# Cosine attention and a gated two-layer product on one Trainium2 core: the last key group's value products in 64 rows, beside the next pair's scores

## The chip, the cores and the metric

The kernel runs on one core of one Trainium2 chip. The metric is the device time of one execution in microseconds (us); a lower one is better. A profile of one execution stands beside it, in which the engines are called PE (TensorE, matrix products), PEld (its loads of stationary operands), DVE (VectorE), ACT (ScalarE), POOL (GpSimd) and SP (SyncE, which issues DMAs). L433 means line 433 of the kernel before.

## What is computed

The inputs are q, k and v of 8 batches, 12 heads, 448 positions and 64 columns, and two weight matrices of 768 x 2048 and 2048 x 768. The reference, cut to what matters:

```python
q_n = q / (norm(q) + 1e-06);  k_n = k / (norm(k) + 1e-06)
scores = matmul(q_n, k_n.T) / tau              # tau = 0.1
attn = exp(scores - max) / sum(exp(scores - max))
x = matmul(attn, v)                            # heads side by side: 3584 x 768
h = x @ w_in
out = (h * clip(h + 3, 0, 6) / 6) @ w_out      # 3584 x 768
```

## The kernel before

The work goes by **pairs** of heads: pair i is batch i // 6 and two heads of it, A and B; there are 48 pairs. Operands of TensorE are bf16, sums are float32 in PSUM.

*Scores* (`scores`, L394) are made transposed: keys stand on the partitions, the 448 queries along the free axis. The 448 keys of a head fall into three blocks of 128 and a rest of 64, which makes four groups of a pair: `GROUPS = [("A0","B0"), ("A1","B1"), ("A2","B2"), ("M",)]`. In groups 0 to 2, each head's product has a contraction of only 64 (the head's columns); A's stands in rows 0 to 63 of the array and B's in rows 64 to 127. Group 3, "M", holds the last 64 keys of both heads, A's on partitions 0 to 63 and B's on 64 to 127; its scores are one product over all 128 rows (from pair 6 on). So a pair then has seven score products, and each takes one PSUM bank.

*Exponentials* (`exps`, L412): ScalarE reads each bank and writes a tile `at` in bf16, seven instructions a pair. Its columns 448 to 511 are set to 1.

*Values* (`values`, L433): the stationary operand is a block of `at`, 128 keys by 128 queries, and the moving one is a block of `vx`, 128 keys by 65 columns: 64 columns of v and a column of ones, whose product is the softmax's sum. There are four blocks of queries, j = 0 to 3. Groups 0 to 2 take eight matmuls of 65 columns each. Group 3 takes four matmuls of 130 columns over all 128 rows: its two blocks of `vx` (slots 3 and 4) hold A's last keys on rows 0 to 63 and zeros below, and zeros above B's on rows 64 to 127. All four groups add up in `PV`, two PSUM banks: bank j // 2 holds two blocks of queries, each with A's 65 columns and B's. `finish_values` (L453, L454, VectorE) divides by the sums and writes `on` in bf16; DMA transposes bring it to `xT`.

*The two layers* run as units between the pairs: `mm1_unit` (L513: six matmuls of 448 columns into a bank, then ACT's relu at L522 and DVE's product at L528 into `gT`) and `mm2_unit` (L549: sixteen matmuls of 384 columns, copied out by ACT at L560 or by DVE at L562 in turn, then stored by DMA).

*The order* of every engine's instructions is written out by hand: an engine takes them in the order in which the program's calls stand. A written list (PLAN) covers pairs 0 to 17, with matmuls on zeros (L615, L620) that fill gaps. From pair FIRST = 18 on a loop does the same for each pair: the next pair's scores of groups 0 to 2, their exponentials, the previous pair's values of groups 1 to 3, `finish_values`, the score and exponential of group 3, the units, with the preparation of later pairs among them, and at the end the pair's own values of group 0.

*The banks.* Two banks are PV's. The six others form a ring that scores and units share in the order of their use (`next_bank`): the first six scores of a pair take all six, the seventh takes the bank of the first again, the first unit after it that of the second. A matmul that opens a bank waits until the last reader of its former content is done.

Of the kernel before, what the change touches and what calls it, by code (L numbers as in the profile page):

```python
# [17 lines left out]
FIRST = 18  # L18
# [43 lines left out]
def kernel(  # L62
# [10 lines left out]
    nc = tc.nc  # L73
    B, H, S, D = q.shape
# [3 lines left out]
    HP = H // 2  # L78
    NP = B * HP
# [50 lines left out]
    PV = psum.tile([128, 2, 512], FP32, name="PV", tag="PV")  # L130
# [13 lines left out]
    def needs(*what):  # L144
        for w in what:
            assert w in issued or any(x < 0 for x in w[1:] if isinstance(x, int)), w
# [217 lines left out]
    GROUPS = [("A0", "B0"), ("A1", "B1"), ("A2", "B2"), ("M",)]  # L364
# [46 lines left out]
            o = at[:, 0 : len(GROUPS[g]), 0:S] if len(x.shape) == 3 else at[:, n, 0:S]  # L411
            nc.scalar.activation(out=o, in_=x, func=AF.Exp, scale=inv_tau)  # L412

    def pv_out(j):
        return PV[:, j // 2, 0:260].rearrange("p (j h e) -> p j h e", j=2, h=2)[:, j % 2, :, :]


    def q_cols(b, j):
        return slice(128 * j, 128 * j + 128)

    def values(i, g):
        needs(("VC", i), ("FI", i - 1), *([("VA", i, g - 1)] if g else []))
        at = at_of.pop((i, g))
        vt = vx[i % NVX]
        last = g == len(GROUPS) - 1
        for n, name in enumerate(GROUPS[g]):
            for j in range(4):
                if name == "M":
                    o, mv = pv_out(j), vt[:, 3:5, :]
                else:  # L430
                    h = "AB".index(name[0])
                    o, mv = pv_out(j)[:, h, :], vt[:, 5 * h + int(name[1]), :]
                nc.tensor.matmul(  # L433
                    o,
                    at[:, n, q_cols(i // HP, j)],
                    mv,
                    start=(name == "A0" and j % 2 == 0),
                    stop=last,
                    skip_group_check=True,
                )  # L440

    twin_on = {}

    def finish_values(i):
        needs(*(("VA", i, g) for g in range(4)))
        if i % 2 == 0:
            needs(("BK", i - 4), ("BK", i - 3))
            twin_on[i // 2] = sb.tile([128, 2, 4, 2, D], BF16, name="on", tag="on", bufs=2)
        rc = sb.tile([128, 2, 4], FP32, name="rc", tag="rc", bufs=2)
        on = twin_on[i // 2][:, i % 2, :, :, :]  # L450
        on_of[i] = on
        pv4 = PV[:, :, 0:260].rearrange("p b (n e) -> p b n e", e=D + 1)
        nc.vector.reciprocal(out=rc[:, :, :], in_=pv4[:, :, :, D])  # L453
        nc.vector.tensor_tensor(  # L454
            out=on[:, :, :, :].rearrange("p (b j) h d -> p b (j h) d", b=2),
            in0=pv4[:, :, :, 0:D],
            in1=rc[:, :, :].to_broadcast([128, 2, 4, D]),
            op=ALU.mult,
        )
# [178 lines left out]
    def whole_units(n):  # L638
# [7 lines left out]
        "LQ": load_qk, "LV": load_v, "W": next_weights, "SQ": square, "RE": reduce, "NO": norms,  # L646
        "NM": normalise, "VC": vcast, "TR": transposes, "XD": crossbar, "XB": back_crossbar, "XP": back_two, "CQ": copy_q, "CK": copy_k, "CS": copy_k3, "SC": scores,
        "EX": exps, "VA": values, "FI": finish_values, "BK": back, "CX": copy_x, "U": unit, "UA": lambda: finish_units("a"), "UV": lambda: finish_units("v"),
        "UU": whole_units, "D": busy, "DP": busy_pv, "OPEN": open_ring,
    }  # L650

    def do(op, *args):
        OPS[op](*args)
        key = (op,) + tuple(a for a in args if isinstance(a, int))
        if op not in ("RE", "NM", "LQ"):
            issued.add(key[:3] if op == "SC" else key)
# [42 lines left out]
    for i in range(FIRST, NP):  # L699
        n_u = len(units[i])  # L700
        even = i % 2 == 0

        def prepare(*what):
            for op, n, *args in what:
                if n < (NP // 2 if op in ("NO", "LV") else NP):
                    do(op, n, *args)

        for g in range(3):
            do("SC", i, g)
        for g in range(3):  # L710
            do("EX", i, g)
        for g in range(1, 4):
            if ("VA", i - 1, g) not in issued:
                do("VA", i - 1, g)
        do("FI", i - 1)
        do("SC", i, 3)
        do("EX", i, 3)

        if (i - 1) % HP > 3:
            do("XB", i - 1)  # L720
        elif even:
            do("XP", i - 2)
        if even:
            prepare(("XD", i + 2))
        do("UU", 1)
        if not even:
            prepare(("CS", i + 1))
        prepare(("SQ", i + 5, "p", 0, 7))
        n = 2
        do("UU", n - 1)  # L730
        if not even:
            prepare(("CK", i + 1), ("CK", i + 2))
        if not even:
            prepare(("NO", (i + 3) // 2))
        do("UU", n_u - n)
        prepare(("NM", i + 3, "p"), ("VC", i + 2, "p"), ("RE", i + 5))
        if even:
            prepare(("XD", i + 3))
        prepare(("LQ", i + 7))
        if not even:  # L740
            prepare(("LV", (i + 5) // 2))
        do("VA", i, 0)
    do("VA", NP - 1, 1)
    do("VA", NP - 1, 2)
    do("VA", NP - 1, 3)
    do("FI", NP - 1)
    do("XB", NP - 1)
    do("UU", len(units[NP]))
# [36 lines left out]
```

## Time and profile before

| what | value |
|---|---|
| time, median of 3 runs | 423.14 us (422.41 to 423.39) |
| span of the profiled execution, first to last instruction | 420.0 us |
| the median less that span | 3.1 us |
| mean granted clock of TensorE | 0.999 |
| matmuls on PE, and what share of the span PE is busy | 3600, 98% |
| values (L433): matmuls, mean length of a record | 1344, 198 ns |
| of them 130 columns wide | 192, 221 ns |

A matmul's record reaches from its start to the modelled end of its results, and the next one starts before that end, so that records overlap: how fast matmuls follow each other is read from their starts. "Idle before" is the time in which an engine did nothing ahead of an instruction, with what ended it. The chain of work that ended last is followed back from the last instruction, at each step to what released it. No more than the span and the three times of runs is known of how the profiled execution stands to the others.

### The profile page before, as it was taken

What the parts mean: (1) busy time and instruction counts of PE and PEld (TensorE: products, weight loads), DVE (VectorE), ACT (ScalarE), POOL (GpSimd) and SP (SyncE); (2) the same over time, 40 slices, a digit from 0 to 9 for tenths busy, and PEclk for the clock granted to TensorE, in tenths of its full rate; (3) what the DMA queues carried; (4) which work ended last, traced back from release to release, by engine and by line L of the source; (5) the groups of instructions that cost most, each with busy time, mean ns of one, the idle gap of its engine ahead of it and who ended that gap; (6) DMA issues with size and microseconds to landing.
All of it is one profiled execution on the core that took longest, in us unless ns stands there. A gap on an engine that the chain in (4) does not pass through costs nothing.

```text
span 420.0 us, 9243 instructions
## 1 busy us (share of the span) xinstructions
PE 412.6 (98%) x3600; PEld 244.6 (58%) x3600; DVE 217.3 (52%) x419; ACT 271.0 (65%) x591; POOL 183.6 (44%) x190
## 2 busy tenths in 40 slices
PE   7999999999999999999999999999999999999996
PEld 5666556556665565555565555555555555655554
DVE  6898677855345654455536454465454443315410
ACT  6899988887558666757747765866765774105400
POOL 7899646444237347257356355365462200000000
PEclk9999999999999999999999999999999999999999
DMA  8999999789796965966885858756953441330033
GB/s 296 311 235 248 182 270 229 154 152 242 202 181 133 190 162 132 179 166 140 190 196 118 191 146 171 186 157 135 193 158 72 85 66 34 70 75 21 0 77 75
DMA packets 91563, 65.29 MB, mean 155 GB/s; under 512 B 56064, under 2 KB 89984, under 8 KB 91520
## 3 DMA queue, kind: packets, MB, share of 16 engines
q1 hardware_dynamic: 87728, 58.37, 59.8%
q0 software_dynamic: 3712, 6.29, 8.6%
q8 instruction: 28, 0.46, 0.5%
q14 instruction: 15, 0.12, 0.1%
q10 hardware_dynamic: 80, 0.05, 0.0%
HBM read 47.19 MB, written 11.01 MB: 139 GB/s over the span
## 4 chain that ended last, share of the span: by engine, by line
PE 96%; DVE 1%; POOL 1%; DMA 1%; ACT 0%; issue 0%; ACTq 0%; DVEq 0%
PE M L513 24%; PE M L549 23%; PE PV L433 12%; PE Z L549 7%; PE M L394 6%; PE Y L513 6%; PE Y L549 6%; PE Z L513 5%; PE Y L394 2%; PE Z L394 1%; PE PV L620 1%; PE SC L394 1%; POOL nrm L246 1%; DMA raw<-in_k_dram 1%; PE Z L291 1%; DVE n L215 0%
## 5 line engine op out<-in xcount | busy, mean ns | idle before, releaser
L549 PEld LDWEIGHTS <-gT 128*128 128x128 bf16 x912 | 88.6, 98 | 58.4
L412 ACT ACTIVATE at<-M 128x448 bf16<-128x448 f32 x199 | 96.8, 567 | 31.2 <-PE M L394 18.9
L513 PEld LDWEIGHTS <-w_in_sb 128*128 128x128 bf16 x768 | 73.7, 98 | 65.8 <-issue 2.7
L513 PE MATMUL M<-xT,w_in_sb 128*128 128x448 bf16 x522 | 107.3, 353 | 0.0
L549 PE MATMUL M<-w_out_sb,gT 128*128 128x384 bf16 (+1 forms) x592 | 99.3, 324 | 0.0
L246 POOL TENSOR_TENSOR nrm<-raw,r 128x896 bf16<-128x896 f32 (+1 forms) x48 | 77.7, 1624 | 43.8 <-ACT r L234 34.7
L528 DVE SCALAR_TENSOR_TENSOR gT<-u,M 128x448 bf16<-128x448 bf16 x87 | 54.0, 620 | 52.3 <-ACT u L522 50.8
L203 POOL TENSOR_TENSOR sq<-raw 128x896 f32<-128x896 f32 (+3 forms) x39 | 63.4, 1627 | 9.9 <-DMA raw<-in_k_dram 4.8
L433 PEld LDWEIGHTS <-at 128*128 128x128 bf16 x1344 | 53.5, 98 | 24.4 <-issue 16.8
L522 ACT ACTIVATE u<-M,bias 128x448 bf16<-128x448 f32 x87 | 56.5, 650 | 16.6 <-PE M L513 15.4
L433 PE MATMUL PV<-vx,at 128*128 128x65 bf16 (+1 forms) x1344 | 64.0, 198 | 0.3 <-DVE on L454 0.2
L215 DVE TENSOR_REDUCE n<-sq 128x14 f32<-128x896 f32 (+1 forms) x50 | 51.8, 1041 | 3.8 <-ACT sq L201 3.6
L351 POOL COPY km<-tT 64x128 bf16<-64x128 bf16 x34 | 9.8, 289 | 96.8 <-DMA tT<-nrm 46.4
L412 ACT ACTIVATE at<-Z 128x448 bf16<-128x448 f32 x48 | 27.1, 565 | 12.5 <-PE M L394 12.4
L560 ACT COPY o<-M 128x384 f32<-128x384 f32 (+1 forms) x19 | 8.9, 470 | 40.5 <-PE M L549 40.4
L562 DVE COPY o<-M 128x384 f32<-128x384 f32 x18 | 10.0, 558 | 47.0 <-PE M L549 32.6
L454 DVE TENSOR_TENSOR on<-PV,rc 128x512 bf16<-128x512 f32 x48 | 33.2, 691 | 1.7
L394 PE MATMUL M<-tT,kz 64*128 64x448 bf16 (+1 forms) x175 | 32.6, 353 | 0.0
L549 PE MATMUL Z<-w_out_sb,gT 128*128 128x384 bf16 (+1 forms) x176 | 29.1, 319 | 0.0
L265 POOL CAST vx<-vr 128x512 bf16<-128x512 f32 x44 | 27.6, 631 | 1.5 <-DMA vr<-in_v_dram 1.5
L453 DVE RECIPROCAL rc<-PV 128x8 f32<-128x8 f32 x48 | 9.9, 207 | 34.9 <-PE PV L433 34.2
L412 ACT ACTIVATE at<-Y 128x448 bf16<-128x448 f32 x47 | 26.7, 569 | 1.7 <-PE Z L394 1.5
(78 smaller groups left out, 352.6 us busy)
## 6 DMA issues: line engine op xcount, KB each, us to landing
vr<-in_v_dram SPq DMA_DIRECT2D x96, 128.0 KB, 4.2
raw<-in_k_dram SPq DMA_DIRECT2D x24, 448.0 KB, 4.4
raw<-in_q_dram SPq DMA_DIRECT2D x24, 448.0 KB, 4.3
out_dram<-o SPq DMA_DIRECT2D x110, 96.0 KB, 2.2
w_in_sb<-in_moe_w_in_dram POOLq DMA_DIRECT2D x4, 768.0 KB, 12.2
w_out_sb<-in_moe_w_out_dram POOLq DMA_DIRECT2D x4, 768.0 KB, 9.2
tT<-nrm SPq DMA_TRANSPOSE x34, 3.3
xT<-on SPq DMA_TRANSPOSE x25, 3.9
```

The source lines that it names most:

```text
L203: engines[e].tensor_tensor(out=o, in0=i, in1=i, op=ALU.mult)
L215: nc.vector.tensor_reduce(out=n2s[d % 2][:, j % 2, c], in_=sq[:, :, :, :].rearrange("p g c d -> p (g c) d")[:, c, :], axis=AX.X, op=ALU.add,)
L246: engines[e].tensor_tensor(out=nrm[:, :, g, :].rearrange("p c g d -> p g c d"), in0=raw_of[j][:, g, :, :], in1=rs[d % 2][3][:, j % 2, :] . ...
L265: (engines[e].copy if e == "a" else engines[e].tensor_copy)(out=o, in_=f)
L394: nc.tensor.matmul(o, ks, qt[rows], start=True, stop=True)
L412: nc.scalar.activation(out=o, in_=x, func=AF.Exp, scale=inv_tau)
L433: nc.tensor.matmul(o, at[:, n, q_cols(i // HP, j)], mv, start=(name == "A0" and j % 2 == 0), stop=last, skip_group_check=True,)
L454: nc.vector.tensor_tensor(out=on[:, :, :, :].rearrange("p (b j) h d -> p b (j h) d", b=2), in0=pv4[:, :, :, 0:D], in1=rc[:, :, :].to_broad ...
L513: nc.tensor.matmul(ps[:, 0:S], w_in_sb[:, cc, fc * 128 : (fc + 1) * 128], x[:, cc, 0:S], start=(cc == 0), stop=(cc == CC - 1),)
L522: nc.scalar.activation(out=u[:, :], in_=ps[:, 0:S], func=AF.Relu, bias=half_bias, scale=1.0 / 6.0)
L528: nc.vector.scalar_tensor_tensor(out=g[:, fc, c0 : c0 + S], in0=u[:, :], scalar=1.0, in1=ps[:, 0:S], op0=ALU.min, op1=ALU.mult,)
L549: nc.tensor.matmul(ps[:, 0:width], lhs, w_out_sb[:, fc, cols], start=(fc == 0), stop=(fc == FCN - 1),)
```

## The change

From pair 18 on, the values of group 3 run as eight matmuls of 65 columns instead of four of 130: A's in rows 0 to 63 of the array, B's in rows 64 to 127, each with its own half of `at` and of `vx`. They are taken out of their place behind groups 1 and 2 and put ahead of the next pair's scores, so that a pair's groups run in the order 0, 3, 1, 2; for the last pair they stand ahead of groups 1 and 2 without scores. `PV` is laid out by head: bank 0 holds A's four blocks of queries, bank 1 B's, and the two halves write different banks; the first matmul of A0 and the first of B0 open their banks. Pairs 0 to 17 keep their order and whole rows, but their group 3, too, takes eight matmuls of 65 columns, since the two heads now lie in two banks. `finish_values` writes `on` in the new order of blocks.

```diff
-    def pv_out(j):
-        return PV[:, j // 2, 0:260].rearrange("p (j h e) -> p j h e", j=2, h=2)[:, j % 2, :, :]
+    def pv_out(j, h):
+        return PV[:, h, (D + 1) * j : (D + 1) * (j + 1)]
+
+    def values_after(i, g):
+        order = [0, 1, 2, 3] if i < FIRST else [0, 3, 1, 2]
+        return [("VA", i, x) for x in order[: order.index(g)][-1:]]
...
     def values(i, g):
-        needs(("VC", i), ("FI", i - 1), *([("VA", i, g - 1)] if g else []))
+        needs(("VC", i), ("FI", i - 1), *values_after(i, g))
...
-        last = g == len(GROUPS) - 1
+        last = g == (3 if i < FIRST else 2)
         for n, name in enumerate(GROUPS[g]):
             for j in range(4):
-                if name == "M":
-                    o, mv = pv_out(j), vt[:, 3:5, :]
-                else:
-                    h = "AB".index(name[0])
-                    o, mv = pv_out(j)[:, h, :], vt[:, 5 * h + int(name[1]), :]
-                nc.tensor.matmul(
-                    o,
-                    at[:, n, q_cols(i // HP, j)],
-                    mv,
-                    start=(name == "A0" and j % 2 == 0),
+                for h in (range(2) if name == "M" else ["AB".index(name[0])]):
+                    rows = slice(64 * h, 64 * h + 64) if name == "M" and i >= FIRST else slice(0, 128)
+                    nc.tensor.matmul(
+                        pv_out(j, h),
+                        at[rows, n, q_cols(i // HP, j)],
+                        vt[rows, 3 + h if name == "M" else 5 * h + int(name[1]), :],
+                        start=(name in ("A0", "B0") and j == 0),
...
         nc.vector.tensor_tensor(
-            out=on[:, :, :, :].rearrange("p (b j) h d -> p b (j h) d", b=2),
+            out=on[:, :, :, :].rearrange("p j h d -> p h j d"),
...
+        if i > FIRST:
+            do("VA", i - 1, 3)
         for g in range(3):
             do("SC", i, g)
...
         do("VA", i, 0)
+    do("VA", NP - 1, 3)
     do("VA", NP - 1, 1)
     do("VA", NP - 1, 2)
-    do("VA", NP - 1, 3)
     do("FI", NP - 1)
```

More of the change, by code (lines that the diff above doesn't have):

```diff
@@ L421, in values @@
     def values(i, g):
-        needs(("VC", i), ("FI", i - 1), *([("VA", i, g - 1)] if g else []))
+        needs(("VC", i), ("FI", i - 1), *values_after(i, g))
         at = at_of.pop((i, g))
         vt = vx[i % NVX]
-        last = g == len(GROUPS) - 1
+        last = g == (3 if i < FIRST else 2)
         for n, name in enumerate(GROUPS[g]):
             for j in range(4):
-                if name == "M":
-                    o, mv = pv_out(j), vt[:, 3:5, :]
-                else:
-                    h = "AB".index(name[0])
-                    o, mv = pv_out(j)[:, h, :], vt[:, 5 * h + int(name[1]), :]
-                nc.tensor.matmul(
-                    o,
-                    at[:, n, q_cols(i // HP, j)],
-                    mv,
-                    start=(name == "A0" and j % 2 == 0),
-                    stop=last,
-                    skip_group_check=True,
-                )
+                for h in (range(2) if name == "M" else ["AB".index(name[0])]):
[5 more added lines that the diff above has]
+                        start=(name in ("A0", "B0") and j == 0),
+                        stop=last,
+                        skip_group_check=True,
+                    )
     twin_on = {}
```

## The prediction

> **What bounds the kernel now.** I read the page first (busy shares, slices, chain), then the timeline of one steady pair.
>
> ```profile
> PE 412.6 (98%) x3600; PEld 244.6 (58%) x3600; DVE 217.3 (52%) x419; ACT 271.0 (65%) x591; POOL 183.6 (44%) x190
> ...
> PE   7999999999999999999999999999999999999996
> ...
> PEclk9999999999999999999999999999999999999999
> ...
> PE 96%; DVE 1%; POOL 1%; DMA 1%; ACT 0%; issue 0%; ACTq 0%; DVEq 0%
> ```
>
> TensorE is the bound nearly from end to end at a full clock, so a step counts only by what it does to the starts of TensorE's matmuls. A busy share hides small holes, because each matmul's record is longer than the step to the next. So I go by starts. The timeline of TensorE around pair 34's scores:
>
> ```profile
> 244.28 0.41 PE L433 MATMUL PV<-vx,at 128*128 128x65 bf16 x8
> 244.62 0.36 PE L394 MATMUL M<-tT,kz 64*128 64x448 bf16 x2
> 244.82 0.35 PE L394 MATMUL Y<-tT,kz 64*128 64x448 bf16 x1
> 244.82 0.35 PE L394 MATMUL Z<-tT,kz 64*128 64x448 bf16 x1
> 245.00 0.35 PE L394 MATMUL M<-tT,kz 64*128 64x448 bf16 x2
> 245.29 0.89 PE L433 MATMUL PV<-vx,at 128*128 128x65 bf16 x20
> 246.02 0.35 PE L394 MATMUL M<-tT,km 128*128 128x448 bf16 x1
> 246.21 0.35 PE L513 MATMUL M<-xT,w_in_sb 128*128 128x448 bf16 x1
> ```
>
> First column start, second length to the last end. The x20 are groups 1 to 3 of the previous pair's values. Their last four are the part that changes, and start at 245.79:
>
> ```profile
> 245.79 0.40 PE L433 MATMUL PV<-vx,at 128*128 128x130 bf16 x4
> ```
>
> From the single starts in these records: values of 65 columns follow each other every 29.4 ns, those of 130 every 57.5 ns, so the last group holds TensorE 4 x 57.5 = 230 ns. The step from the last value at 244.490 to the first score at 244.616 is 126 ns, of which 96 are the change from 128 rows to 64; the change back costs 282 - 187 = 95. Two scores in different halves start 3 ns apart and share 187 ns: the halves do run together.
>
> Next, who holds the banks. The ring has six, a pair's first six scores take all, so the seventh score (246.02) needs the first exponential and the first unit (246.21, L513) the second. ScalarE, same stretch:
>
> ```profile
> 244.48 0.48 ACT L560 COPY o<-M 128x384 f32<-128x384 f32 x1 [1.48 <-PE M L549]
> 245.01 0.98 ACT L412 ACTIVATE at<-M 128x448 bf16<-128x448 f32 x2
> ```
>
> The second exponential ends at 245.99, 0.22 before the unit: cover today. In the next pair the unit's output ahead of the scores is copied by VectorE, and this is late:
>
> ```profile
> 252.41 0.56 DVE L562 COPY o<-M 128x384 f32<-128x384 f32 x1 [1.31 <-PE M L549]
> ```
>
> ```profile
> 252.94 0.35 PE L394 MATMUL Z<-tT,kz 64*128 64x448 bf16 x1
> 253.03 0.35 PE L394 MATMUL M<-tT,kz 64*128 64x448 bf16 x1
> ```
>
> These two should start together. The second waits for the copy (end 252.97, plus 0.055) and loses 84 ns. Of the 29 pairs from 19 to 47, 17 are of this kind (D) and 12 of the other (A).
>
> **The change, part by part.**
>
> (1) Last group, pairs 18 to 46 (29 of them, run at the head of iterations 19 to 47): four matmuls of 130 columns become eight of 65, two by two on the halves, each with its own weight load. No row here has 65 columns in 64 rows. Lower bound: the 65-column step per couple. Upper: the halves don't overlap, 8 x 29.4, and beyond that 12 ns for each load left uncovered (the first score couple after a change of rows steps 200 instead of 188), 331 ns in all. I take the lower: at 244.612 and 244.615 two half loads start, their matmuls 4 ns after each, and the next two loads at 244.627 and 244.630, so loads of two halves run together and a matrix accepts a next load after 15 ns, half the step. With the first steps after a change as they are behind 245.290 (39, 35, 30, 30): 134 ns.
>
> The page "TensorE: Matmul & The Clock Gate" of the Trainium skill, section "LDWEIGHTS (loading the stationary operand)", gives a load of 128 columns as 128/1.2 = 107 ns; by it four more loads, if nothing covered them, would be an estimated 29 x 4 x 107 ns = 12.4 us of loss. The 29.4 ns step above, with a load in every one, speaks against that.
>
> (2) Its place. The group leaves the stretch between scores and seventh score (-230) and goes ahead of the scores (+134). The two changes of rows remain two. Two consequences count from the last value of group 0 to the first unit's start. Now: A 246.208 - 244.490 = 1.718; D 254.222 - 252.426 = 1.796.
> After, by TensorE alone: 126 + 134 to the first score, 188 + 189 between scores, 281 to the values, 497 for sixteen, 189 for the seventh: 1.604. The D wait goes: the last scores come at 126 + 134 + 377 = 637 ns, the bank is free at 600.
> After, by the bank: first score at 260, the second exponential's end 1.375 later as now (245.991 - 244.616), less 11 because the first score is then no longer the first after the change (349 instead of 360 ns), plus 52 from ScalarE's end to TensorE's start (an exponential that ended at 32.406 let a score start at 32.458): 1.676. This is the later one: **the unit waits 72 ns for its bank in every pair**. Behind it in TensorE's queue stands everything else. The seventh score needs the first exponential, which has over 0.2 us in hand.
> Gain: A 0.042 x 12 = 0.50; D 0.120 x 17 = 2.04; together 2.54 us.
>
> (3) Pair 47 has no scores to stand next to: two changes of rows more, 96 + 95 + 134 - 230 = +0.09 us.
>
> (4) Pairs 0 to 17: whole rows, but by head: eight of 65 (235 ns) for four of 130 (230), 18 x 5 ns = +0.09 us at most, nothing where TensorE waits in the first 40 us.
>
> (5) Waits. The moved group's first load waits for its exponential; the previous seventh ended about 248.17, four us before the next values: nothing. VectorE's normalisation (L454, 691 ns) now writes in runs of 64. GpSimd writes such runs (L246, 1624 ns) as fast as whole rows (L203, 1627): I take nothing; doubled it would cost 1.4 us at most, since only two of the 48 (20.93 and 28.41) stand on the chain. DMAs, SP's and GpSimd's orders stay as they are.
>
> Sum: -2.54 + 0.09 + 0.09 = -2.36 us, of a span of 420.0: 417.6. The median 423.1 lies 3.1 above that span, which I keep: **420.8 us**.
>
> **Rivals.** With S for the last group's length, a unit starts at 1.676 + (S - 0.134).
> - R1, couples overlap in part, 45 ns each, S 0.19: A +0.014, D -0.064, in all -0.92 + 0.18: 422.4. For it: four instructions per 30 ns have no row. Against: six in 18 ns around 244.62.
> - R2, the other side: the halves take turns, because the loads or the short matmuls of two halves don't run together, S 0.25. Then the scores come 116 ns later still, and with them exponential and unit: A +0.074 x 12, D about 0: +0.82 + 0.18, **424.1**. It decides from 54 ns per couple on, where the sum is zero. The change would not do what it says. Fully uncovered loads (S 0.331) would give 426.5. Against both: the two loads 3 ns apart.
> - R3, no bank wait (ScalarE starts earlier, or lets go earlier than its record's end): 1.604, A -0.114, D -0.192, in all -4.63 + 0.18: 418.7. Against: waits for ScalarE and VectorE came 52 and 55 ns behind the record.
>
> **How the numbers follow.** Forecast 0.66; R1 0.11; R2 0.13; R3 0.07; worse still (up to 426.5) 0.03. Range: R3 and R1 with half a microsecond of scatter (the runs lie from 422.41 to 423.39) on the low side and a little above R1 on the high, 418.4 to 422.8; 0.16 lies above. A difference under 0.2% (0.85 us) can't be told from none; R1 falls there, so faster 0.73, same 0.11, slower 0.16.
>
> **What would show it.** In a pair's timeline: the eight 64-row values before the scores, couples about 30 ns apart (60 means R2); no second start like 253.03; the 130-column rows gone; and the first L513 behind the seventh score 0.26 instead of 0.19 after it, about 0.05 behind the second exponential's end (0.19 means R3). If the couples step 30 ns and the time still doesn't fall, a wait that I haven't listed has come.

## The result and the profile after

The changed kernel takes 420.15 us (median of 13 runs, 419.46 to 422.87) against 422.96 us of before in the same comparison (13 runs): a ratio of 0.9944, with an interval of 0.9928 to 0.9959, that is 2.4 us less (1.7 to 3.0). A ratio in this document is taken over all the runs of a comparison, so it isn't the quotient of the two medians (which differ by 2.8 us here). The forecast was 2.36 us less, 420.8 us.

The page of the profile after, its lines that answer to those of before:

```profile
PE 411.0 (98%) x3792; PEld 242.1 (58%) x3792; DVE 214.5 (51%) x419; ACT 268.3 (64%) x591; POOL 183.8 (44%) x190
...
PE   7999999999999999999999999999999999999996
...
PEclk9999999999999999999999999999999999999999
...
PE 97%; DVE 1%; DMA 1%; issue 0%; ACT 0%; ACTq 0%
```

TensorE is still the bound at a full clock, and nothing here tells that the kernel has changed: 192 matmuls more, the same share. What changed stands in the starts. The timeline of TensorE around pair 34's scores (start, length):

```profile
244.20 0.63 PE L434 MATMUL PV<-vx,at 128*128 128x65 bf16 x16
244.67 0.35 PE L394 MATMUL M<-tT,kz 64*128 64x448 bf16 x2
244.86 0.35 PE L394 MATMUL Y<-tT,kz 64*128 64x448 bf16 x1
244.86 0.35 PE L394 MATMUL Z<-tT,kz 64*128 64x448 bf16 x1
245.05 0.35 PE L394 MATMUL M<-tT,kz 64*128 64x448 bf16 x2
245.33 0.66 PE L434 MATMUL PV<-vx,at 128*128 128x65 bf16 x16
245.83 0.35 PE L394 MATMUL M<-tT,km 128*128 128x448 bf16 x1
246.08 0.54 PE L514 MATMUL M<-xT,w_in_sb 128*128 128x448 bf16 x2
```

The first line holds two kinds, eight values of group 0 over 128 rows and eight of group 3 in 64. A narrower window of the same timeline shows the second kind alone:

```profile
244.54 0.29 PE L434 MATMUL PV<-vx,at 64*128 64x65 bf16 x8
```

From 244.54 to the first score at 244.67 the whole group takes 0.13 us, where its four wide matmuls took 0.23. The four couples start 38, 36 and 29 ns after each other, and the two halves of a couple 2 to 4 ns apart. ScalarE in the same stretch:

```profile
245.06 0.98 ACT L412 ACTIVATE at<-M 128x448 bf16<-128x448 f32 x2 [0.18 <-PE M L394]
```

The second exponential ends at 246.04, and the unit (L514) starts at 246.08; exactly, 51 ns behind. The step from the seventh score to the unit is 0.25 us instead of 0.19. That is the wait for the bank. And in the next pair, whose unit ahead of the scores is copied by VectorE, the last two scores now start together:

```profile
252.94 0.35 PE L394 MATMUL Z<-tT,kz 64*128 64x448 bf16 x1
252.94 0.35 PE L394 MATMUL M<-tT,kz 64*128 64x448 bf16 x1
```

One thing in this profile was in no sum. In pair 19 the timeline of TensorE has a hole, the only one after the first 30 us:

```profile
126.07 1.11 PE L514 MATMUL M<-xT,w_in_sb 128*128 128x448 bf16 x5
128.02 1.29 PE L514 MATMUL M<-xT,w_in_sb 128*128 128x448 bf16 x6 [0.84 <-DMA xT<-on]
```

The unit's sixth matmul waits for the transposed output of pair 17. SP's queue in that execution:

```profile
101.58 3.64 SPq L302 DMA_TRANSPOSE tT<-nrm  x1
...
124.17 1.22 SPq L486 DMA_TRANSPOSE xT<-on  x1
```

An issue that took 1.35 us before took 3.64, and all that stands behind it in SP's order came later, the needed one at 124.17 instead of 119.80. The hole makes the stretch from this unit to the next group 0 7.22 us long, where the like pairs take 6.21: 1.0 us. With it the span is 418.7 us, 1.3 less than the 420.0 of before, although the comparison of many runs gives 2.4. Whether the hole belongs to the change is asked in the last experiment.

### The profile page after: what moved, and what is told of

Its sections match the earlier page's. It is cut to its first block, busy times and chain, and to the rows that moved or that the text cites. A ratio compares the mean times of both kernels' runs of the same rounds, so it can differ in the third digit from the quotient of the medians.

```text
span 418.7 us, 9613 instructions
## 1 busy us (share of the span) xinstructions
PE 411.0 (98%) x3792; PEld 242.1 (58%) x3792; DVE 214.5 (51%) x419; ACT 268.3 (64%) x591; POOL 183.8 (44%) x190
## 4 chain that ended last, share of the span: by engine, by line
PE 97%; DVE 1%; DMA 1%; issue 0%; ACT 0%; ACTq 0%
PE M L514 24%; PE M L550 23%; PE PV L434 12%; PE Z L550 7%; PE Y L514 6%; PE Y L550 6%; PE Z L514 6%; PE M L394 5%; PE PV L621 3%; PE Y L394 1%; PE Z L394 1%; PE SC L394 1%; DMA xT<-on 1%; PE Z L291 1%; PE Y L616 1%; PE SC L391 0%
## 5 line engine op out<-in xcount | busy, mean ns | idle before, releaser
L514 PEld LDWEIGHTS <-w_in_sb 128*128 128x128 bf16 x768 | 73.3, 97 | 68.7 <-issue 8.2
L514 PE MATMUL M<-xT,w_in_sb 128*128 128x448 bf16 x522 | 107.2, 352 | 0.8 <-DMA xT<-on 0.8
L529 DVE SCALAR_TENSOR_TENSOR gT<-u,M 128x448 bf16<-128x448 bf16 x87 | 52.8, 619 | 56.5 <-ACT u L523 56.3
L434 PEld LDWEIGHTS <-at 128*128 128x128 bf16 (+1 forms) x1536 | 54.8, 97 | 24.6 <-issue 15.4
L523 ACT ACTIVATE u<-M,bias 128x448 bf16<-128x448 f32 x87 | 55.3, 659 | 15.6 <-PE M L514 15.5
L394 PE MATMUL M<-tT,kz 64*128 64x448 bf16 (+1 forms) x175 | 31.3, 351 | 0.0
L514 PE MATMUL Y<-xT,w_in_sb 128*128 128x448 bf16 x126 | 27.3, 352 | 0.0
```

Source lines behind the costliest of these rows:

```text
L394: nc.tensor.matmul(o, ks, qt[rows], start=True, stop=True)
L434: nc.tensor.matmul(pv_out(j, h), at[rows, n, q_cols(i // HP, j)], vt[rows, 3 + h if name == "M" else 5 * h + int(name[1]), :], start=(name ...
L514: nc.tensor.matmul(ps[:, 0:S], w_in_sb[:, cc, fc * 128 : (fc + 1) * 128], x[:, cc, 0:S], start=(cc == 0), stop=(cc == CC - 1),)
L523: nc.scalar.activation(out=u[:, :], in_=ps[:, 0:S], func=AF.Relu, bias=half_bias, scale=1.0 / 6.0)
L529: nc.vector.scalar_tensor_tensor(out=g[:, fc, c0 : c0 + S], in0=u[:, :], scalar=1.0, in1=ps[:, 0:S], op0=ALU.min, op1=ALU.mult,)
```

## The experiments

My theory was the sum of the prediction: the halves shorten the group by 100 ns; each change of rows costs some 95; and ahead of the first unit there are two chains, TensorE's own starts and the exponentials' bank, of which the later counts. Its rivals: that the place alone made the gain, by pushing the scores behind the copy that they wait for; or that the halves alone made it.

**Halves without the move.** Group 3 in 64 rows, but in its old place:

```diff
-        order = [0, 1, 2, 3] if i < FIRST else [0, 3, 1, 2]
+        order = [0, 1, 2, 3]
...
-        last = g == (3 if i < FIRST else 2)
+        last = g == 3
...
-        if i > FIRST:
-            do("VA", i - 1, 3)
         for g in range(3):
             do("SC", i, g)
...
-    do("VA", NP - 1, 3)
     do("VA", NP - 1, 1)
     do("VA", NP - 1, 2)
+    do("VA", NP - 1, 3)
     do("FI", NP - 1)
```

> Halves without the move: group 3 in 64 rows, but in its old place behind groups 1 and 2. Times against 422.96 us for before; 0.26 us are counted for pairs 0 to 17, as the profile of the change shows them. My theory (halves shorten the group to 134 ns, but every change of rows costs 96 in and 95 out, and the bank chain decides the first unit): each of 30 pairs gets two more changes of rows, +96 +95 +134 -230 = +95 ns, so +2.85 +0.26 = +3.1 us, 426.1 us; the late second score of 84 ns in 17 pairs stays, no wait for the second exponential. Rival H (the shorter group is the whole gain, its place does nothing): -110 ns in 30 pairs, 419.9 us. Rival P (the place is the whole gain, by pushing the scores behind the copy they wait for): 423.2 us.

Measured: 425.45 us against 422.76, ratio 1.0066 (1.0040 to 1.0091), 2.8 us more. The timeline of TensorE around pair 35's scores:

```profile
254.90 0.35 PE L394 MATMUL Z<-tT,kz 64*128 64x448 bf16 x1
254.98 0.35 PE L394 MATMUL M<-tT,kz 64*128 64x448 bf16 x1
255.26 0.89 PE L434 MATMUL PV<-vx,at 128*128 128x65 bf16 x24
256.08 0.36 PE L394 MATMUL M<-tT,km 128*128 128x448 bf16 x1
256.28 0.54 PE L514 MATMUL M<-xT,w_in_sb 128*128 128x448 bf16 x2
```

The x24 are sixteen values over 128 rows and the group's eight in 64. The late score is there (254.98 behind 254.90), and from the first value to the seventh score it is 0.82 us where it was 0.73: the group is shorter by 0.1 and pays 0.19 for going into 64 rows and out again. The unit starts 1.90 us after the last value of group 0 in the pairs with the late score and 1.82 in the others, against 1.80 and 1.72. By themselves the halves lose; the rival "halves only" falls, with 419.9 us, and so does "place only", with 423.2. The page "TensorEngine Tiling (Array Packing)" of the Trainium skill, section "Key Properties", says that a change of the tiling mode drains TensorE. This run shows a price at each change, 0.19 us for the two, but not the drain itself: the first half starts 128 ns after the last whole-row value, whose record is 190 ns or more long, so by the modelled ends the two still overlap.

**The move without the halves.** Group 3 ahead of the scores, over whole rows:

```diff
-                    rows = slice(64 * h, 64 * h + 64) if name == "M" and i >= FIRST else slice(0, 128)
+                    rows = slice(0, 128)
```

> The move without the halves: group 3 at the head of the iteration, eight matmuls of 65 columns over whole rows. My theory: the group takes 250 ns ahead of the change of rows, the first score comes 376 ns after the last value of group 0, and the first unit 1.375 + 0.052 us after that by its bank, 1.803 in every pair, against 1.718 (12 pairs) and 1.796 (17 pairs) before: +1.02 +0.12 +0.26 = +1.4 us, 424.4 us, with a wait of some 70 ns for the second exponential and no late second score. Rival P (place only): 17 late scores of 84 ns gone, -1.43 +0.26, 421.8 us. Rival H (halves only): 423.2 us.

Measured: 423.57 us against 422.76, ratio 0.9994 (0.9973 to 1.0016). By the medians the run is 0.8 us longer than before, near "halves only" (423.2) and below the forecast (424.4); by the ratio it equals before, and the forecast (1.003) and "place only" (421.8, 0.997) lie outside the interval or at its end. The times alone would favour "halves only". The trace shows what happened. TensorE and ScalarE around pair 34's scores:

```profile
245.45 0.36 PE L394 MATMUL M<-tT,kz 64*128 64x448 bf16 x2
...
246.12 0.66 PE L434 MATMUL PV<-vx,at 128*128 128x65 bf16 x16
246.63 0.35 PE L394 MATMUL M<-tT,km 128*128 128x448 bf16 x1
246.88 0.35 PE L514 MATMUL M<-xT,w_in_sb 128*128 128x448 bf16 x1
```

```profile
245.85 0.98 ACT L412 ACTIVATE at<-M 128x448 bf16<-128x448 f32 x2 [0.30 <-PE M L394]
```

In the next pair, the kind that had the late score, the last two scores start together:

```profile
253.85 0.35 PE L394 MATMUL Z<-tT,kz 64*128 64x448 bf16 x1
253.86 0.35 PE L394 MATMUL M<-tT,kz 64*128 64x448 bf16 x1
```

The bank wait is there (exponential to 246.83, unit at 246.88), the late score is gone, and the unit comes 1.798 to 1.802 us after the last value of group 0, in both kinds of pairs, against 1.803 forecast. The group has R2's length here, 250 ns instead of 132, and the move then gains nothing.

The forecast of +1.4 us can be followed by starts in the two traces. From the last value of group 0 to the unit the 29 pairs add up to 52.19 us against 51.20 before, +1.0 (forecast 1.14, since a pair with the late score lost 1 ns where 7 were forecast, and the others 81 where 85 were); pairs 0 to 17 cost the 0.26; and between the unit and the next group 0 some 0.08 us come back, 3 ns a pair. Together that is +1.2 us. The spans differ by 0.9 only, because the profiled execution of before took 0.17 us more between pairs 25 and 26 than in like pairs, and because the two executions start and end a little apart. Why the times of the runs show less still isn't known; I put it down to their scatter, which isn't shown. "Halves only" falls by the trace, since it has neither the bank wait nor the late score's going.

**Between the scores.** Halves as in the change, but between the second and third couple of scores:

```diff
-        if i > FIRST:
-            do("VA", i - 1, 3)
         for g in range(3):
+            if i > FIRST and g == 2:
+                do("VA", i - 1, 3)
             do("SC", i, g)
```

> Halves, but between the second and the third couple of scores instead of ahead of all. My theory: the first score comes 126 ns after the last value of group 0 as before the change, so the second exponential's bank is free at 126 + 1375 + 52 = 1.553 us, while TensorE itself reaches the first unit at about 1.608; the last scores come at about 637 ns, behind the copy at 600. Neither wait is left, 1.608 against 1.675 in the changed kernel, -0.067 x 29 = -1.9 us against it: 0.990 of before, about 418.7 us. Rival (the bank wait in the changed kernel is only a symptom, ScalarE holds the pair's pace further on): as the changed kernel, 0.994.

Measured: 418.41 us against 422.76, ratio 0.9883 (0.9853 to 0.9914). TensorE and ScalarE around pair 35's scores:

```profile
250.67 0.41 PE L434 MATMUL PV<-vx,at 128*128 128x65 bf16 x8
251.01 0.55 PE L394 MATMUL M<-tT,kz 64*128 64x448 bf16 x3
251.21 0.35 PE L394 MATMUL Y<-tT,kz 64*128 64x448 bf16 x1
251.40 0.28 PE L434 MATMUL PV<-vx,at 64*128 64x65 bf16 x8
251.52 0.35 PE L394 MATMUL Z<-tT,kz 64*128 64x448 bf16 x1
251.52 0.35 PE L394 MATMUL M<-tT,kz 64*128 64x448 bf16 x1
251.81 0.66 PE L434 MATMUL PV<-vx,at 128*128 128x65 bf16 x16
252.30 0.35 PE L394 MATMUL M<-tT,km 128*128 128x448 bf16 x1
252.49 0.54 PE L514 MATMUL M<-xT,w_in_sb 128*128 128x448 bf16 x2
```

```profile
251.41 0.98 ACT L412 ACTIVATE at<-M 128x448 bf16<-128x448 f32 x2 [2.50 <-PE M L394]
```

The exponential ends at 252.39, 0.10 ahead of the unit, which now follows the seventh score at TensorE's own step of 0.19; the last two scores start together. Both waits are gone, and the unit comes 1.61 us after the last value of group 0 (forecast 1.608; 1.675 in the changed kernel); over the 29 pairs that is 1.9 us less, as forecast. A pair that took 7.89 us takes 7.83. So the bank wait was a cost of its own, and not a sign of ScalarE's pace: the rival falls.

**Behind the scores.** The same, but after the third couple:

```diff
-        if i > FIRST:
-            do("VA", i - 1, 3)
         for g in range(3):
             do("SC", i, g)
+        if i > FIRST:
+            do("VA", i - 1, 3)
```

> Halves, behind the third couple of scores, still inside the 64-row stretch. My theory: no wait for the second exponential (1.553 against 1.608 us), but the late second score of 84 ns is back in 17 pairs: 1.608 in 12 pairs, 1.692 in 17, so -0.80 +0.29 = -0.5 us against the changed kernel, 0.993 of before. Rival (any place inside the 64-row stretch is as good): equal to the place between the scores, 0.990.

Measured: 419.20 us against 422.76, ratio 0.9911 (0.9877 to 0.9944), 0.8 us slower than between the scores by the medians of one chip. The intervals of the two overlap; the trace shows the difference, here around pair 35's scores:

```profile
251.88 0.35 PE L394 MATMUL Z<-tT,kz 64*128 64x448 bf16 x1
251.97 0.35 PE L394 MATMUL M<-tT,kz 64*128 64x448 bf16 x1
252.07 0.95 PE L434 MATMUL PV<-vx,at 64*128 64x65 bf16 x24
252.87 0.35 PE L394 MATMUL M<-tT,km 128*128 128x448 bf16 x1
253.06 0.54 PE L514 MATMUL M<-xT,w_in_sb 128*128 128x448 bf16 x2
```

The x24 are the group's eight values in 64 rows and sixteen over 128. The late score is back, and with it the unit at 1.685 us in such pairs, while the others stand at 1.61 (forecast 1.692 and 1.608). Inside the 64-row stretch the place is not free: ahead, the group pushes the exponentials; behind, it leaves the scores too early for the copy; between, it does neither.

**The two small losses taken back.** Between the scores, with pairs 0 to 17 in the old layout with four matmuls of 130 columns, and the last pair's group 3 at the end over whole rows:

```diff
-    def pv_out(j, h):
-        return PV[:, h, (D + 1) * j : (D + 1) * (j + 1)]
+    def pv_out(i, j, h):
+        n = 2 * j + h if i < FIRST else 4 * h + j
+        return PV[:, n // 4, (D + 1) * (n % 4) : (D + 1) * (n % 4 + 1)]
...
-        order = [0, 1, 2, 3] if i < FIRST else [0, 3, 1, 2]
+        order = [0, 1, 2, 3] if i < FIRST or i == NP - 1 else [0, 3, 1, 2]
...
+                if name == "M" and i < FIRST:
+                    c = 2 * (D + 1) * (j % 2)
+                    nc.tensor.matmul(
+                        PV[:, j // 2, c : c + 2 * (D + 1)],
+                        at[:, n, q_cols(i // HP, j)],
+                        vt[:, 3:5, :],
...
-                    rows = slice(64 * h, 64 * h + 64) if name == "M" and i >= FIRST else slice(0, 128)
+                    rows = slice(64 * h, 64 * h + 64) if name == "M" and i < NP - 1 else slice(0, 128)
...
-        if i > FIRST:
-            do("VA", i - 1, 3)
         for g in range(3):
+            if i > FIRST and g == 2:
+                do("VA", i - 1, 3)
             do("SC", i, g)
...
-    do("VA", NP - 1, 3)
     do("VA", NP - 1, 1)
     do("VA", NP - 1, 2)
+    do("VA", NP - 1, 3)
```

> The place between the scores, and the two terms that the change loses elsewhere taken back: pairs 0 to 17 keep the old layout and four matmuls of 130 columns, and the last pair's group 3 stays at the end in whole rows. My theory: 14 ns in each of 18 pairs, 0.26 us, and 0.08 us at the end come back beside the 1.9 us of the place: 418.1 us, 0.987 to 0.988 of before; in the profile the group takes 230 ns again in the early pairs, and the last pair has no change of rows. Rival (the early pairs have slack that hides 14 ns each): as the place between the scores alone, 418.4 us. The clock of runs can hardly tell 0.3 us, the profile can.

Measured: 417.70 us (417.55 to 418.13) against 422.88, ratio 0.9880 (0.9856 to 0.9904), the lowest time of all versions. Against the place between the scores alone (418.41) the time can't tell. In the traces, from the first score to pair 18's first score it is 102.93 us in the changed kernel and 102.67 here, as before the change (102.68); from the last pair's first value to the unit behind them 0.98 us here, 1.07 in the changed kernel, 0.96 before. So the early pairs don't have the slack to hide it, and their rival falls. The values by form, the narrow ones in 64 rows and the wide ones over whole rows (instructions, busy time, mean record):

```profile
L446 PE MATMUL PV<-vx,at 64*128 64x65 bf16 x232 | 8.2, 190 | 0.0
L435 PE MATMUL PV<-vx,at 128*128 128x130 bf16 x72 | 7.1, 222 | 0.0
```

These are 29 pairs with eight in halves and 18 with four wide ones, as meant.

**The changed kernel once more.**

> The changed kernel as it is, profiled once more. Its first profile has one wait of 0.84 us for the transposed attention output in pair 19, which no sum of mine holds. If it is chance (SP's queue late in that execution), this profile is without it and its span about 417.7 us; if it belongs to the change, it is there again, and the span 418.5 or more.

Measured: 419.42 us, a span of 417.3. The waits of TensorE in this profile:

```profile
PE PV L621 <- DVE vx L674: 2.5, 1, 2.5
PE Z L291 <- POOL nrm L246: 0.3, 1, 0.3
PE PV L434 <- DVE on L455: 0.2, 1, 0.2
```

No wait for `xT` is among them, nor is there one in the five other experiments' profiles. So the hole isn't a fixed part of the change; how often it comes isn't known. SP's queue varies here too: one transpose of `tT` takes 2.60 us where its like took 1.26 before, and the needed issue comes at 121.82, 2.0 us later than before, which TensorE doesn't feel. Why the transpose took 3.64 us in the first profile isn't settled; no run took that queue's load away.

## Why the prediction was right

The time came within a microsecond of the forecast, and for the reasons given, step by step. That the gain agrees so closely (2.4 us, forecast 2.36) is in part luck: by starts the place gained 0.17 us more than its term, and pairs 0 to 17 lost 0.17 more than theirs.

1. **The group's length.** 134 ns forecast, 132 measured: couples start 38, 36 and 29 ns apart, and the first score 29 ns later. The lower bound was right, loads and matmuls of two halves run together. R1 (45 ns a couple) and R2 (60) fall.
2. **The place.** 1.676 us forecast from the last value of group 0 to the first unit; 1.674 to 1.676 in each of the 29 pairs. That the pairs come alike out of two unlike ones (1.72 and 1.80 before) is the plainest mark: a chain that starts at the first score has taken over. The unit starts 50 to 52 ns behind the second exponential's end, so R3 (no bank wait) falls too. The unit waits 61 to 66 ns, where 72 were forecast. From pair to pair it is 0.126 us less in the pairs with a late score and 0.047 in the others, 2.71 us in all against 2.54 forecast: 0.123 and 0.044 up to the unit, and 3 ns behind it. The stretch from the unit to the next group 0 is 3 ns shorter in every version whose unit waits for its bank; why isn't settled.
3. **The last pair.** +0.09 forecast, +0.10 measured (0.96 to 1.07 us).
4. **Pairs 0 to 17: the one step that was mis-sized.** 0.09 us "at most" was forecast, from eight steps of 29.4 ns against 230; it was 0.26 (102.68 to 102.93 us), 14 ns in each pair. Eight whole-row matmuls that go to and fro between the two heads' banks take 250 ns, 31 each (the move without the halves shows them alone: steps of 29 and 33 in turn), which is some 20 ns more a pair; by the two traces part of it is made up again in the first 42 us. The 29.4 ns was misread: it is the short step, which most matmuls take, but every third or fourth step is 32 to 36 ns, and in the rows of before that the prediction read group 0 steps 30.4 ns in the mean. I had called a bound what was the best row.
5. **Waits.** VectorE's normalisation takes 692 ns against 691, as assumed, and the moved group's own wait costs nothing.

The forecast of the time carried one more assumption, that the 3.1 us between span and median stay. In the later runs each time lies 2.1 us above its own span, so the profiled execution of before was a quick one of its kind; the difference between two kernels isn't touched by that. Had I gone by the spans of two single executions, the hole in pair 19 would have made 1.3 us of a gain of 2.4.

What the prediction saw and didn't follow: it named the bank wait of 72 ns a pair as a cost of the place. The same table of starts says where the group should stand, between the second and third couple, where both chains are short; that is worth about as much again as the change (0.9883 after 0.9944).

## What to carry to other kernels

Where one engine is busy all the time, read its starts, not its share, and write down for the next shared point every chain that leads there with its length; a step that shortens one chain gains only down to the next one. A matmul that needs half the rows belongs into a stretch that already runs in halves (here 2.8 us lost outside it, 2.4 gained inside); and within that stretch, put it where it delays nothing that others wait for and fills the time of what you wait for yourself. Size a new form by the mean and the worst of the near rows too, when the text says "at most".

## What the runs showed of the hardware

- Two matmuls of 65 columns, each with its own load of 64 x 128, run in the two halves of the array in about the step of one: 29 to 38 ns a couple, 1 to 4 ns apart in the changed kernel. Only this case, in which they write two banks, was run.
- Going from 128 rows to 64 and back costs 0.19 us together, beyond the normal steps, whether matmuls of 65 or of 448 columns stand at the border: 125 to 129 ns from a whole-row value to the first matmul in halves, 120 to 124 from the last short couple to a whole-row matmul, 282 from the last couple of scores, where 29, 28 and 187 are the steps without a change.
- Whole-row matmuls of 65 columns that alternate between two banks step 29 and 33 ns in turn, 31 in the mean. Where they change the bank after four, the mean is 30.2 to 30.4, with single steps of 32 to 36 ns among those of 29.
- A wait of TensorE for ScalarE ends 50 to 52 ns behind the end of ScalarE's record, in all pairs from 19 on of all versions in which it was the later chain; a wait for VectorE's copy ends 53 to 55 ns behind it.
